# Input transpositions from TensorE to VectorE, and two groups of small products in four 64x64 tiles, in a linear-attention plus expert-mixture kernel

## The chip, the cores and the metric

One core of one Trainium2 chip. The metric is the time on the device in microseconds (us), the median of several runs. The profile names the engines PE (TensorE), PEld (TensorE's weight loads), DVE (VectorE), ACT (ScalarE), POOL (GpSimd) and SP (SyncE).

## The reference, cut to what matters

```python
# r, k, v, w, a, b: (B=4, H=8, S=768, D=40), fp32
for t in range(S):
    y[:, :, t] = einsum('bhd,bhde->bhe', rt, state)
    Sa = einsum('bhde,bhe->bhd', state, at)
    state = state * wt[:, :, None, :] - einsum('bhd,bhe->bhde', Sa, bt) \
          + einsum('bhd,bhe->bhde', vt, kt)
x = y.transpose(0, 2, 1, 3).reshape(3072, 320)
# four experts, F = 1024
p = domain_probs / (domain_probs.sum(-1, keepdims=True) + 1e-09)
for e in range(4):
    out += p[:, e:e+1] * (relu(x @ w1[e]) @ w2[e])
```

## The kernel before: the parts that matter

The 768 tokens are taken in 12 chunks of 64. Inside a chunk the recurrence becomes triangular products (E, F, C, X below), a 64x64 inverse whose 32x32 half is solved on VectorE, and a few products with the state. A **unit** is two batches of one chunk: 8 pairs of heads, 24 units. Chunks are grouped in seven **blocks** of 1, 2, 2, 2, 2, 2, 1.

The expert products of the block before are cut into pieces, and `mix(us)` puts some us' worth of them into TensorE's instruction stream. TensorE's order is fixed by hand: it is the order of the program. The order of the other engines is chosen when the kernel is built, and is fixed from then on.

Inputs come as one run of 40 floats (160 bytes) for each token, and TensorE turns them, into PSUM:

```python
by.dma_start(out=n[:, :, 0:D], in_=src[0].rearrange("h t e -> t h e"))

def turn(x):
    p = bank("p" + x)
    for j in range(NJ):                       # 4 transpositions on TensorE
        nc.tensor.transpose(out=p[:, j*P:(j+1)*P],
            in_=nat[x][:, 2*j:2*j+2, :].rearrange("p h e -> p (h e)"), identity=ident[:])
    return p
```

E and F, and C and X, are pairs of products that share the moving operand; one product of 64 rows by 128 columns does both:

```python
def triangles(u):                             # E/F
    for m in range(M):                        # M = 8
        for s in range(2):
            nc.tensor.matmul(out=pef[s][:, m*L:(m+1)*L],
                lhsT=KNT[half(s), m].rearrange("p x t -> p (x t)"), rhs=u.AE[half(s), s, m, :], ...)
# ... in step(): C/X
            nc.tensor.matmul(out=pc[s][:, m*L:(m+1)*L],
                lhsT=VST[half(s), i, j*P:(j+1)*P], rhs=u.R[half(s), m, :], ...)
```

The order of a block:

```python
def attention(b, after):
    us = b.units
    stage(us[0], 1)
    for y, u in enumerate(us):
        stage(u, 2)                           # turn NK, KN, A; scale
        if y + 1 < len(us):
            stage(us[y + 1], 1)               # turn W, scan, reciprocal of the next unit
        mix(4.3)
        stage(u, 3)                           # triangles
        mix(2.2)
        stage(u, 4)                           # natural
    ...
    solve()                                   # VectorE, 32 us or so
    mix(56)
    # ... inverse, then the steps of each chunk, then the gather for the experts
```

## Time and profile before

| | before |
|---|---|
| time, median of 3 (range) | 1390.56 us (1390.23 to 1391.24) |
| span of the profiled run | 1389.3 us |
| end of the first and the second solve on VectorE | 79.6, 198.1 us |
| TensorE after 198.1 us: occupied, idle | 1136.5, 50.0 us |

TensorE's "occupied" time is counted in its own instruction order: from the start of one record to the start of the next, less the part in which it demonstrably did nothing. I use it rather than the listed means of single products because products overlap (in the timeline quoted in the prediction the group of E/F listed with 1.89 us from 726.87 on ends 0.16 us after the next group has started, at 728.60). The profile lines themselves are in the prediction below; one more is needed later, the queue of the input loads (packets, MB, share of 16 DMA engines).

### The profile page before, as it was taken

What the parts mean: (1) busy time and instruction counts of PE and PEld (TensorE: products, weight loads), DVE (VectorE), ACT (ScalarE), POOL (GpSimd) and SP (SyncE); (2) the same over time, 40 slices, a digit from 0 to 9 for tenths busy, and PEclk for the clock granted to TensorE, in tenths of its full rate; (3) what the DMA queues carried; (4) which work ended last, traced back from release to release, by engine and by line L of the source; (5) the groups of instructions that cost most, each with busy time, mean ns of one, the idle gap of its engine ahead of it and who ended that gap; (6) DMA issues with size and microseconds to landing.
All of it is one profiled execution on the core that took longest, in us unless ns stands there. A gap on an engine that the chain in (4) does not pass through costs nothing.

```text
span 1389.3 us, 26523 instructions
## 1 busy us (share of the span) xinstructions
PE 1250.1 (90%) x11680; PEld 869.5 (63%) x11680; DVE 624.7 (45%) x898; ACT 283.9 (20%) x609; POOL 88.7 (6%) x123
## 2 busy tenths in 40 slices
PE   5076779999999989999989999989999989899998
PEld 5075658866567666567666567666567765466676
DVE  8854573566403657303566403465603369011000
ACT  2022212132131131131122131122131221120111
POOL 4000010000100000100000100000100001000010
PEclk8568889999999999999999999989999999899999
DMA  7214634555223554243453333464214440414363
GB/s 123 54 21 73 110 84 97 116 110 109 76 49 87 103 102 90 48 87 87 95 111 62 76 78 68 95 126 75 66 50 93 90 110 12 102 39 105 95 151 86
DMA packets 216722, 118.42 MB, mean 85 GB/s; under 512 B 181985, under 2 KB 200481, under 8 KB 216609
## 3 DMA queue, kind: packets, MB, share of 16 engines
q0 software_dynamic: 17600, 73.46, 21.4%
q1 hardware_dynamic: 194720, 42.63, 18.1%
q8 instruction: 92, 1.51, 0.5%
q10 hardware_dynamic: 4288, 0.66, 0.4%
q14 instruction: 22, 0.17, 0.0%
HBM read 108.84 MB, written 7.86 MB: 84 GB/s over the span
## 4 chain that ended last, share of the span: by engine, by line
PE 74%; DVE 13%; DMA 6%; issue 5%; ACT 1%; SPq 1%; POOL 0%; DVEq 0%; POOLq 0%; ACTq 0%
PE ph L481 27%; PE po L493 23%; DVE tmp L287 3%; PE pef L223 3%; PE pc L414 3%; DMA natW<-in_w_dram 3%; DMA w1s<-in_moe_w_dram 2%; PE py L426 2%; DVE Y L291 2%; PE pa L375 2%; PE pSN L347 2%; PE py L432 2%; PE pt L385 2%; PE pVST L347 2%; DVE Xl L291 1%
## 5 line engine op out<-in xcount | busy, mean ns | idle before, releaser
L481 PE MATMUL ph<-xT,w1s 64*128 64x512 f32 (+1 forms) x2240 | 453.2, 548 | 31.7 <-DVE osb L502 9.4
L493 PE MATMUL po<-w2s,hs 128*128 128x320 f32 x1536 | 435.0, 441 | 0.0
L493 PEld LDWEIGHTS po<-w2s,hs 128*128 128x128 f32 x1536 | 292.1, 193 | 124.3 <-issue 10.4
L481 PEld LDWEIGHTS ph<-xT,w1s 64*128 64x128 f32 x2240 | 223.7, 193 | 223.7 <-issue 194.6
L487 ACT ACTIVATE hs<-ph 128x512 f32<-128x512 f32 (+1 forms) x224 | 111.0, 534 | 687.3 <-PE ph L481 686.7
L502 DVE SCALAR_TENSOR_TENSOR osb<-po,gate,osb 128x320 f32<-128x320 f32 x72 | 39.5, 550 | 339.5 <-PE po L493 339.1
L199 DVE RECIPROCAL GI<-G 128x512 f32<-128x512 f32 x24 | 80.5, 3353 | 0.8
L467 POOL DMA_DIRECT2D w1s<-in_moe_w_dram x56 | 37.8, 679 | 571.9 <-PE ph L481 571.7
L230 ACT COPY F<-pef 32x512 f32<-32x512 f32 x96 | 45.1, 469 | 102.2 <-PE pef L223 101.0
L353 DVE COPY SN<-pSN 128x512 f32<-128x512 f32 x24 | 16.6, 692 | 108.4 <-PE pSN L347 108.4
L232 DVE TENSOR_TENSOR AE<-pef,mask 64x512 f32<-64x512 f32 x48 | 33.1, 689 | 64.9 <-ACT F L230 64.6
L471 POOL DMA_DIRECT2D w2s<-in_moe_w_dram x28 | 26.0, 928 | 538.2 <-PE po L493 530.4
L223 PEld LDWEIGHTS pef<-AE,KNT 64*128 64x128 f32 x768 | 50.0, 198 | 14.6 <-issue 10.3
L223 PE MATMUL pef<-AE,KNT 64*128 64x64 f32 x768 | 51.5, 282 | 5.0 <-DVE KNT L210 3.5
L176 PE MATMUL pW<-ident,natW 128*128 128x128 f32 x96 | 18.8, 330 | 34.8 <-DMA natW<-in_w_dram 29.4
L414 PEld LDWEIGHTS pc<-R,VST 64*128 64x128 f32 x768 | 44.9, 188 | 5.6 <-issue 4.1
L414 PE MATMUL pc<-R,VST 64*128 64x64 f32 x768 | 45.7, 272 | 1.1 <-DVE RV__99 L407 1.1
L325 PE MATMUL pi<-F 32*32 32x32 f32 x768 | 14.2, 195 | 32.1 <-DVE F L310 32.1
L420 DVE TENSOR_TENSOR CX<-pc,mask 128x512 f32<-128x512 f32 x48 | 30.7, 686 | 27.3 <-PE pc L414 27.2
L192 ACT COPY w_shift<-pW 128x512 f32<-128x512 f32 x24 | 14.0, 585 | 130.7 <-PE pW L176 121.2
L437 DVE TENSOR_TENSOR Yo<-py,G 128x512 f32<-128x512 f32 x24 | 16.6, 692 | 53.2 <-PE py L432 53.2
L176 PEld LDWEIGHTS pW<-ident,natW 128*128 128x128 f32 x96 | 12.8, 166 | 38.2 <-issue 32.4
(104 smaller groups left out, 1097.1 us busy)
## 6 DMA issues: line engine op xcount, KB each, us to landing
w1s<-in_moe_w_dram POOLq DMA_DIRECT2D x56, 640.0 KB, 7.6
w2s<-in_moe_w_dram POOLq DMA_DIRECT2D x28, 1280.0 KB, 7.1
xT<-yD SPq DMA_DIRECT2D x24, 320.0 KB
natW<-in_w_dram SPq DMA_DIRECT2D x48, 80.0 KB
natA<-in_a_dram SPq DMA_DIRECT2D x48, 80.0 KB
yD<-Yo SPq DMA_DIRECT2D x48, 80.0 KB
out_dram<-osb SPq DMA_DIRECT2D x48, 80.0 KB
natR<-in_r_dram SPq DMA_DIRECT2D x44, 80.0 KB
```

The source lines that it names most:

```text
L199: nc.vector.reciprocal(out=u.GI[:], in_=u.G[:, :, 1:L + 1])
L223: nc.tensor.matmul(out=pef[s][:, m * L:(m + 1) * L], lhsT=KNT[half(s), m].rearrange("p x t -> p (x t)"), rhs=u.AE[half(s), s, m, :], start ...
L230: nc.scalar.copy(out=F_[r, u.m, 0:L - z * Q], in_=cut(pef[s][r])[:, :, z * Q:L])
L287: nc.vector.tensor_tensor(out=m, in0=in0[:, :, None, :].to_broadcast([P, n0, n1, nr]), in1=in1[:, None, :, :].to_broadcast([P, n0, n1, nr] ...
L291: nc.vector.tensor_reduce(out=out, in_=m, axis=AX.X, op=ALU.add, negate=negate)
L347: nc.tensor.transpose(out=p[:, j * P:(j + 1) * P], in_=t[:, i, j].rearrange("p s d -> p (s d)"), identity=ident[:],)
L414: nc.tensor.matmul(out=pc[s][:, m * L:(m + 1) * L], lhsT=VST[half(s), i, j * P:(j + 1) * P], rhs=u.R[half(s), m, :], start=True, stop=True,)
L467: nc.gpsimd.dma_start(out=w1s[half(d)], in_=moe_w1[e, :, d * (F // 2):(d + 1) * (F // 2)].rearrange("(k p) f -> p k f", p=64),)
L481: nc.tensor.matmul(out=ph[d][:, 0:n], lhsT=w1s[half(d), k_, f * P:(f + 1) * P], rhs=xT[half(d), k_, 0:n], start=(k_ == 0), stop=(k_ == NK ...
L487: nc.scalar.activation(out=hs[-1][1][:, 0:n], in_=ph[d][:, 0:n], func=ACTF.Relu)
L493: nc.tensor.matmul(out=po[:, 0:DM], lhsT=h[:, tt * P:(tt + 1) * P], rhs=w2s[:, f, :], start=(x == 0), stop=(x == NF - 1),)
L502: nc.vector.scalar_tensor_tensor(out=osb[tt][:], in0=po[:, 0:DM], scalar=sc, in1=osb[tt][:], op0=ALU.mult, op1=ALU.add,)
```

## The change

The intent is to take work off TensorE, which was busy 90% of the span.

1. Inputs are loaded as runs of four tokens (640 bytes; two tokens and 320 bytes in the blocks of one chunk), straight into the rows from which VectorE's transposition in squares of 32x32 turns them. As 40 is more than 32, each input is loaded twice, the second copy shifted by 32 elements. TensorE's 20 input transpositions per unit, their PSUM banks and ScalarE's copies of two of the five (W and R) go.
2. E/F and C/X are written as 64x64 products in four tiles of the array, twice as many instructions.
3. The order changes: whole pairs of units are prepared at once; the turns of the next block are ordered behind the solve, which then runs uninterrupted; from the fourth load of a block on, loads are issued after the previous block's gather; the credits of `mix` are new (14 ahead of each pair's E/F, 50 beside the solve).

```diff
+    def turn(x, b, p, out):
+        nq = 2 * b.n
+        n = natural_tile(b.n)
+        end = M * nq * D
+        b.loads += 1
...
+            if b.before and b.loads > 3:
+                order.enter_context(tc.issue_after(b.before.gathered))
             for s in range(2):
+                src = srcs[x][s][2*p:2*p+2, s::2, b.t, :].rearrange("i j (r q) e -> r (i j) (q e)", q=nq)
+                for d in range(2):
+                    by = nc.scalar if b.cs[0] == p == 0 and s == 1 else nc.sync
+                    o = Q * (1 - d)
+                    by.dma_start(out=n[SL[s]+Q*d : SL[s]+Q*d+Q, o:o+end].rearrange("r (x e) -> r x e", e=nq*D), in_=src)
+        with ExitStack() as order:
+            if solved:
+                order.enter_context(tc.issue_after(solved[-1]))
+            nc.vector.transpose(
+                out=out.rearrange("p c m (r q) -> p m q c r", q=nq),
+                in_=n[:, Q:Q+end].rearrange("p (m q e) -> p m q e", q=nq, e=D)[:, :, :, 0:Q].rearrange(
+                    "p m q (c r) -> p m q c r", c=b.n))
...
-                nc.tensor.matmul(
-                    out=pef[s][:, m*L:(m+1)*L], lhsT=KNT[half(s), m].rearrange("p x t -> p (x t)"),
-                    rhs=u.AE[half(s), s, m, :], start=True, stop=True)
+                for x in range(2):
+                    nc.tensor.matmul(
+                        out=pef[s][half(x), m*L:(m+1)*L], lhsT=KNT[rows(s), m, x, :],
+                        rhs=u.AE[rows(s), s, m, :], start=True, stop=True)
...
-            nc.tensor.matmul(out=pc[s][:, m*L:(m+1)*L], lhsT=VST[half(s), i, j*P:(j+1)*P],
-                rhs=u.R[half(s), m, :], start=True, stop=True)
+            for x in range(2):
+                nc.tensor.matmul(out=pc[s][half(x), m*L:(m+1)*L],
+                    lhsT=VST[rows(s), i, j*P+x*L : j*P+(x+1)*L], rhs=u.R[rows(s), m, :], start=True, stop=True)
...
     def attention(b, after):
+        for p in range(NP):
+            if p >= b.early:
+                decays(b, p)                  # turn W, scan, reciprocal
+            scaled(b, p)                      # turn NK, KN, A; scale
+            if not start:
+                turned_r(b, p)
+            mix(14)
+            for u in pairs[p]:
+                triangles(u)
             mix(4.3)
+            for u in pairs[p]:
+                natural(u)
...
         solve()
+        if start:                             # first block: the rest waits until the solve is done
+            for p in range(NP):
+                turned_r(b, p)
+            decays(after, 0)
...
-        mix(56)
+        mix(50)
```

Cut: the multiplications now read SBUF for pairs of units, G has two buffers of pairs instead of four of units, the mask is built by GpSimd, the accumulator `osb` has four buffers instead of five.

## The prediction

> **What bounds the kernel now.** I read the page first: the busy times, the 40 slices and the costliest groups.
>
> ```profile
> PE 1250.1 (90%) x11680; PEld 869.5 (63%) x11680; DVE 624.7 (45%) x898; ACT 283.9 (20%) x609; POOL 88.7 (6%) x123
> ...
> PE   5076779999999989999989999989999989899998
> ...
> DVE  8854573566403657303566403465603369011000
> ```
>
> TensorE is busy for 1250 of 1389 us. It is idle in the first seven slices (243 us); after that each slice is 80% to over 90% full. VectorE works in bursts and never fills a late slice. Next I read the view of stretches, to separate the start from the steady part.
>
> ```profile
> 35.00:70.00 35.00, 1.09 (x4) 0.71 (x4) 28.42 (x50) 0.58 (x1) 0.00 (x0) 0.50 0.26 50
> ...
> 140.00:175.00 35.00, 27.69 (x202) 22.28 (x200) 19.62 (x43) 8.34 (x21) 2.27 (x3) 0.85 0.62 114
> ...
> 600.00:780.00 180.00, 169.85 (x1648) 115.81 (x1646) 95.61 (x136) 40.10 (x84) 8.73 (x11) 0.97 0.42 85
> ```
>
> The columns after the length are PE, PEld, DVE, ACT and POOL busy, then clock and DMA share. So there are two regimes. **At the start** the first 32x32 solve runs alone on VectorE (TensorE works 1.1 of 35 us). **Later**, TensorE is 94% busy and any TensorE time taken out of its instruction order shortens the run. The timeline shows what the affected groups occupy in that order; I take start to start of the next group, not the listed mean, because matmuls overlap.
>
> ```profile
> 726.87 1.89 PE L223 MATMUL pef<-AE,KNT 64*128 64x64 f32 x32
> 728.60 4.51 PE L481 MATMUL ph<-xT,w1s 64*128 64x512 f32 x20
> ...
> 733.98 0.60 PE L176 MATMUL pR<-ident,natR 128*128 128x128 f32 x4
> 734.41 0.60 PE L176 MATMUL pNK<-ident,natNK 128*128 128x128 f32 x4
> ...
> 825.34 1.13 PE L375 MATMUL pa<-RV__98,AE 128*64 128x40 f32 x32
> 826.29 1.11 PE L375 MATMUL pa<-RV__99,AE 128*64 128x40 f32 x32
> ```
>
> Four input transposes take 734.41 - 733.98 = 0.43 us; the 32 E/F products of a unit 1.73 us (54 ns each; 1.94 us in a slower place). The C/X products (L414) take 3.6 us for two units. The view of waits, of TensorE alone, also shows TensorE waiting for inputs, because an input must land before its transposition can leave TensorE's fixed order:
>
> ```profile
> PE pi L325 <- DVE F L310: 32.1, 1, 32.1
> PE pW L176 <- DMA natW<-in_w_dram: 29.4, 10, 9.3
> PE ph L481 <- DVE osb L502: 9.4, 1, 9.4
> ...
> PE pR L176 <- DVE AE L232: 7.0, 8, 1.7
> ```
>
> [...]individual records in L414 start in pairs 6 ns apart, the next pair 112 ns after the first (128 columns[...]); with 64-column weights (L385, L375) the pairs come every 58 ns[...]. [...]No group of the kernel before uses four at once, but L426 runs two row tiles together and L375 two column tiles together (start gaps of 7 and 51 ns), so both directions are seen to overlap. [...]1024 elements in 1.92 us (the solve's transposition of F)[...]. I use 1.9 to 2.1 us.
>
> **The change, part by part.** A unit is two batches of one 64-token chunk; there are 24 of them, in seven blocks (1, 2, 2, 2, 2, 2, 1 chunks).
>
> *Transpositions leave TensorE.* Five inputs x 0.435 us = 2.17 us per unit, with their ScalarE copies (w_shift and R, 28 us in all), which bound nothing.
>
> *Four tiles.* E/F goes from 16 pairs x 112 ns = 1.79 us to 16 groups of four x 58.5 ns = 0.94 us per unit; the instruction count doubles, to 15 ns apart, which L325 nearly shows already (128 in 2.15 us, 16.8 ns). C/X gains the same. Together 1.7 us per unit. So TensorE loses 3.9 us per unit, 93 us over all 24 units, but only those after the start count in full.
>
> *VectorE gains.* 50 transpositions of 1024 elements at 2.0 us and 20 of 512 at 1.05 us = 121 us. The multiplications read SBUF in place of PSUM and are paired: 24 of 1024 elements at 1.22 us (rate of the solve's 1024-element products) against 48 at 0.68; AE similar. Reciprocals (80 us) and scans (30 us) stay. VectorE goes from 625 to about 740 us, 58% of the new span: no bound on average.
>
> *DMA.* Each input is loaded twice, 19.7 to 39.3 MB, but in runs of 640 bytes (four tokens) rather than 160, so about 72,000 packets in place of 123,000. The hardware queue's share should stay near 16 to 18%. I count no gain or loss.
>
> *Start up to the end of the second block's solve (0 to 198 us in the timeline).* The first solve ran from 31.8 to 79.6 us, with two scans, two reciprocals and a 5 us wait for the next block's W inside. The change orders the next turns behind the solve: it then lasts about 34 us (35.2 less four other evictions of 0.5 us in the steady block at 744.7). VectorE's new chain before it (turn 1.05, scan 1.24, reciprocal 3.35, two turns, product 1.22, turn, two AE at 0.69, all twice) puts its start near 32 us, as before, so it ends near 66. The steps take 27 us, as before, plus some 4 us of waits behind the postponed W and R work: gather near 97 us (before: about 107). Block two then needs on VectorE: turns 14, scan and reciprocal 9, products 10, masks 3 and 33 us of solve, plus evictions and landing: solve ends near 175 us instead of 198. Gain **23 us**.
>
> *From there to the end.* TensorE loses 18 units x 3.9 + 4 units x 0.86 (C/X only) = **74 us**. Idle there was about 55 us, 8 of some 10 us per block being input landings, which TensorE no longer waits for directly. But the new chain after a block's last step (G has two buffers, so the next W turn cannot start earlier) is turn 2 + scans 2.5 + reciprocal 6.7 + product 2.45 + turn 2 + AE 2.45 = 18 us, about 20 with evictions, against some 15 us of expert products scheduled in its shadow; the second pair is 27 us against 24. So I expect 5 to 8 us of idle per steady block in place of 10: gain **8 us**, chosen from a possible -15 to +35. The solve (34 us, under 55 us of scheduled products) has room to spare.
>
> Sum: 1390 - 23 - 74 - 8 = **1285 us**.
>
> **Rivals.** *VectorE becomes the bound.* For it: 120 us of VectorE work per steady block, in runs of 20 to 27 us that TensorE must wait for, and step evictions (0.5 to 0.7 us) queue behind 6.7 us reciprocals. Against: the period stays near 195 us, and the schedule now gives 14 units of credit before each pair. If all such runs were uncovered, 20 us per block more: 1370 to 1390 us. *Column tiles do not load beside each other when row tiles do too.* For: no group before runs four at once. Against: the pair gaps above. Then E/F and C/X stay at 1.8 us per unit: 37 us lost, about 1320 us. *The waits vanish altogether*, as no transposition sits in TensorE's order any longer and the credits were retuned: 25 to 35 us better, about 1255 us. *Doubled bytes delay expert weights*: the last blocks already wait 9 us for w1s; 5 to 15 us worse.
>
> **Range and chances.** 1285 us; low 1250 from the vanishing waits with a little more at the start, high 1322 from the failed four-tile overlap or 7 more us of idle per block. To stay within 2% (above 1363 us) VectorE would have to eat nearly everything saved: 0.05; slower 0.02; faster 0.93.
>
> **What would show it.** In the profile after: about 11,700 + 1536 - 480 matmuls, PE busy near 1160 us; E/F and C/X near 15 ns from start to start (30 refutes); STREAM_TRANSPOSE of 128x1024 near 2.0 us, VectorE near 740 us; the first solve ended near 66 us and the second near 175; TensorE's waits for natW gone and waits of E/F for VectorE's AE or KNT there, 2 to 5 us each. The prediction fails if those waits exceed 15 us per block, or a transposition takes over 3 us.

1390 - 23 - 74 - 8 = 1285 us is worked out from figures (pairs of records 112 and 58 ns apart, 0.43 us for four transpositions, 1.92 us for 1024 elements on VectorE). That two pairs can run side by side as four tiles was the author's estimate from those gaps; nothing in the kernel before shows four at once.

## More of the kernel before

From the page of the kernel before:

```profile
q1 hardware_dynamic: 194720, 42.63, 18.1%
```

## The result

| | before | after | difference |
|---|---|---|---|
| time, median of 4 (range) | 1390.9 (1390.23 to 1396.01) | 1310.99 (1308.56 to 1317.53) | |
| ratio, 95% interval | | 0.9425 (0.9385 to 0.9466) | |
| span of the profiled run | 1389.3 | 1309.8 | -79.5 |
| end of the second solve | 198.1 | 188.4 | -9.7 |
| TensorE occupied after that | 1136.5 | 1073.8 | -62.7 |
| TensorE idle after that | 50.0 | 42.9 | -7.1 |

A ratio is the mean time of one kernel's runs over that of the other's of the same rounds, so it is not quite the ratio of the medians quoted here. The three last rows add up to the difference of the spans: -9.7 - 62.7 - 7.1 = -79.5.

The page of the kernel after: busy times and counts, two rows of the 40 slices, and the queue of the input loads.

```profile
PE 1169.0 (89%) x12736; PEld 805.1 (61%) x12736; DVE 720.9 (55%) x966; ACT 260.4 (20%) x561; POOL 92.7 (7%) x128
...
PE   2067679979899989999989999989999999999998
...
DVE  7995883579803388913389913369913355702000
...
q1 hardware_dynamic: 144192, 62.13, 23.0%
```

TensorE lost 81 us of busy time (1250.1 to 1169.0) with 1056 more instructions, and VectorE gained 96. VectorE now has full slices, about one per block, and after the start the slices beside them on TensorE still read 9: its bursts lie mostly beside products. The input queue moves half as much again with a quarter fewer packets, and its packets took a larger share of time, 23.0 against 18.1%.

The view of stretches of the kernel after (length; PE, PEld, DVE, ACT, POOL busy; clock; DMA share; GB/s), for the same three stretches as in the prediction:

```profile
35.00:70.00 35.00, 2.60 (x90) 2.52 (x92) 33.39 (x55) 1.92 (x6) 1.89 (x2) 1.00 0.50 104
...
140.00:175.00 35.00, 28.75 (x276) 22.80 (x276) 30.70 (x56) 8.66 (x22) 2.28 (x3) 0.79 0.42 95
...
600.00:780.00 180.00, 173.97 (x1833) 114.33 (x1832) 113.39 (x142) 36.84 (x75) 9.79 (x13) 0.97 0.47 109
```

In the steady 180 us TensorE is busier than before (173.97 against 169.85): it does the same work in a shorter period. VectorE has gone from 95.6 to 113.4 us. In the first stretch VectorE is nearly full (33.4 of 35 us, 28.4 before): the solve runs without interruption. (This trace holds no record of the clock before 75.95 us, so the 1.00 of the first stretch is not a measurement.)

The timeline of TensorE after, for E/F and C/X (start, length in us; engine; line; operation; tiles; count; wait):

```profile
117.88 2.10 PE L277 MATMUL pef<-AE__113,KNT 40*64 40x64 f32 x128
119.91 2.43 PE L543 MATMUL ph<-xT,w1s 64*128 64x256 f32 x20
...
221.68 2.15 PE L472 MATMUL pc<-R,VST 40*64 40x64 f32 x128
223.75 2.43 PE L543 MATMUL ph<-xT,w1s 64*128 64x256 f32 x20
```

From 117.88 to 119.91 us 128 records of E/F take 2.03 us, 15.9 ns each; C/X takes 2.07 us, 16.2 ns. After the first four, single records start in fours, 6 to 7 ns apart, each four 58 ns behind the one before; in the kernel before, the records of L375 and L385 came in pairs 58 ns apart. So all four tiles run at once. (Each fp32 product appears as two records, so 128 records are the 64 products of two units.)

The waits of TensorE after (waited us, times, longest):

```profile
PE pef L277 <- DVE AE__113 L260: 39.7, 12, 14.1
...
PE ph L543 <- DMA xT<-yD: 16.4, 7, 6.9
PE pef L277 <- DVE AE__114 L260: 16.4, 7, 12.0
PE ph L543 <- DMA w1s<-in_moe_w_dram: 9.2, 5, 3.1
...
PE pVST L403 <- ACT VS__107 L451: 5.8, 1, 5.8
```

The waits for `natW` are gone. In their place E/F waits for AE, which is the end of VectorE's new chain. Expert products also wait longer for the gather (xT, 7.8 us before, 16.4 now). That chain at the boundary of a steady block, from the timeline of VectorE after:

```profile
460.72 2.01 DVE L203 STREAM_TRANSPOSE G<-nat__75 128x1024 f32<-128x1024 f32 x1
463.18 2.35 DVE L239 TENSOR_TENSOR_SCAN G<-G,first 128x520 f32<-128x520 f32 x2
465.56 6.55 DVE L243 RECIPROCAL GI<-G 128x1024 f32<-128x1024 f32 x1
...
472.39 2.35 DVE L253 TENSOR_TENSOR KNT<-KNT,GI 128x1024 f32<-128x1024 f32 x2
...
477.14 2.47 DVE L260 TENSOR_TENSOR AE__113<-AT,G 40x1024 f32<-40x1024 f32 x2
```

From 460.72 to 479.61 us is 18.9 us; and TensorE at the end of it, with the clock of the same time from the view of stretches:

```profile
478.50 0.33 PE L277 MATMUL pef<-AE__113,KNT 40*64 40x64 f32 x4 [3.02 <-DVE AE__113 L260]
479.75 3.43 PE L277 MATMUL pef<-AE__113,KNT 40*64 40x64 f32 x115 [0.92 <-DVE AE__113 L260]
...
485.18 10.71 PE L543 MATMUL ph<-xT,w1s 64*128 64x512 f32 x40
```

```profile
478.00:489.00 11.00, 8.02 (x138) 5.61 (x140) 7.31 (x8) 3.76 (x8) 0.00 (x0) 0.53 0.88 216
489.00:500.00 11.00, 11.00 (x60) 5.55 (x60) 10.93 (x5) 3.48 (x8) 0.00 (x0) 1.00 0.35 87
```

TensorE waited 3.02 + 0.92 us, and a granted clock of a half was recorded for 10.2 us (478.7 to 489.0 us): 115 records of E/F in 3.43 us are 29.8 ns each, against 15.9 ns at 117.88 us, where the granted clock was 1.00. So the wait costs more than its own length: E/F is the group that runs right behind it.

Two more blocks show the same: waits of 2.45 and 0.77 us go with a granted clock of 0.5 for 10.2 us (676.69 to 686.93 us), waits of 3.13 and 0.92 us with 6.8 us of it (878.08 to 884.91). At 676.69 us the record of the clock falls 0.24 us before the first wait, of 2.45 us, ends at 676.93, and so before the second wait began. (The profile models where a product ends, so the length of a wait is not exact.) Before the second pair of another block E/F waited 0.63 and 0.92 us (from 310.06 us on), and the granted clock stayed at 1.00.

### The profile page after: what moved, and what is told of

Its sections match the earlier page's. It is cut to its first block, busy times and chain, and to the rows that moved or that the text cites. A ratio compares the mean times of both kernels' runs of the same rounds, so it can differ in the third digit from the quotient of the medians.

```text
span 1309.8 us, 28541 instructions
## 1 busy us (share of the span) xinstructions
PE 1169.0 (89%) x12736; PEld 805.1 (61%) x12736; DVE 720.9 (55%) x966; ACT 260.4 (20%) x561; POOL 92.7 (7%) x128
## 3 DMA queue, kind: packets, MB, share of 16 engines
q1 hardware_dynamic: 144192, 62.13, 23.0%
## 4 chain that ended last, share of the span: by engine, by line
PE 63%; DVE 14%; issue 13%; DMA 6%; POOL 2%; SPq 1%; ACT 1%; DVEq 0%; POOLq 0%
PE ph L543 24%; PE po L555 21%; DMA w1s<-in_moe_w_dram 2%; PE pef L277 2%; PE pa L432 2%; PE pc L472 2%; PE pSN L403 2%; PE pt L442 2%; PE pVST L403 2%; DVE tmp L342 2%; PE py L484 1%; PE py L490 1%; DMA xT<-yD 1%; DVE AT L203 1%; DVE KNT L203 1%
## 5 line engine op out<-in xcount | busy, mean ns | idle before, releaser
L543 PE MATMUL ph<-xT,w1s 64*128 64x512 f32 (+1 forms) x2240 | 465.8, 555 | 32.6 <-DMA xT<-yD 16.4
L543 PEld LDWEIGHTS ph<-xT,w1s 64*128 64x128 f32 x2240 | 250.2, 196 | 215.6 <-issue 184.0
L243 DVE RECIPROCAL GI<-G 128x1024 f32<-128x1024 f32 (+1 forms) x14 | 78.9, 5638 | 0.3
L277 PE MATMUL pef<-AE__113,KNT 40*64 40x64 f32 x896 | 24.3, 273 | 41.3 <-DVE AE__113 L260 39.7
L277 PEld LDWEIGHTS pef<-AE__113,KNT 40*64 40x64 f32 x896 | 21.9, 183 | 47.4 <-DVE AE__113 L260 26.8
L495 DVE TENSOR_TENSOR Yo<-py,G 128x512 f32<-128x512 f32 x24 | 16.5, 687 | 51.1 <-PE py L490 41.2
L342 DVE TENSOR_TENSOR tmp<-Y,Tl 128x1024 f32<-128x1024 f32 (+2 forms) x49 | 35.7, 729 | 1.7
L346 DVE TENSOR_REDUCE Y<-tmp 128x32 f32<-128x256 f32 (+3 forms) x49 | 35.5, 724 | 1.7
L346 DVE TENSOR_REDUCE Xl<-tmp 128x32 f32<-128x128 f32 (+3 forms) x49 | 35.5, 724 | 1.6
L409 DVE COPY SN<-pSN 128x512 f32<-128x512 f32 x24 | 16.5, 689 | 34.9 <-PE pSN L403 34.9
L381 PEld LDWEIGHTS pi<-F 32*32 32x32 f32 x768 | 13.4, 111 | 35.1 <-issue 30.9
L286 DVE TENSOR_TENSOR AE__113<-pef,mask 64x512 f32<-64x512 f32 x28 | 19.3, 689 | 26.4 <-ACT F L284 21.9
L472 PEld LDWEIGHTS pc<-R,VST 40*64 40x64 f32 x1536 | 25.0, 135 | 12.3 <-issue 12.2
```

The source lines that it names most:

```text
L243: nc.vector.reciprocal(out=b.GI, in_=G[:, :, :, 1:L + 1])
L277: nc.tensor.matmul(out=pef[s][half(x), m * L:(m + 1) * L], lhsT=KNT[rows(s), m, x, :], rhs=u.AE[rows(s), s, m, :], start=True, stop=True,)
L342: nc.vector.tensor_tensor(out=m, in0=in0[:, :, None, :].to_broadcast([P, n0, n1, nr]), in1=in1[:, None, :, :].to_broadcast([P, n0, n1, nr] ...
L346: nc.vector.tensor_reduce(out=out, in_=m, axis=AX.X, op=ALU.add, negate=negate)
L472: nc.tensor.matmul(out=pc[s][half(x), m * L:(m + 1) * L], lhsT=VST[rows(s), i, j * P + x * L:j * P + (x + 1) * L], rhs=u.R[rows(s), m, :], ...
L543: nc.tensor.matmul(out=ph[d][:, 0:n], lhsT=w1s[half(d), k_, f * P:(f + 1) * P], rhs=xT[half(d), k_, 0:n], start=(k_ == 0), stop=(k_ == NK ...
```

## The experiments

**Theory.** Both removals pay as predicted. What is missing against the prediction (26 us) should lie (a) at the start, where the second block's A comes late, and (b) in the waits of E/F for VectorE's chain and the slow clock behind them. **Rivals.** The four tiles give nothing by themselves; the transpositions alone do all; VectorE's load is the new limit; the doubled bytes cost time.

All runs were timed in three rounds. The kernel before had medians of 1390.7, 1393.0, 1391.3 and 1393.0 us. Unless said otherwise a result was correct.

### 1. The four tiles alone, in the kernel before

```diff
-  nc.tensor.matmul(out=pef[s][:, m*L:(m+1)*L], lhsT=KNT[half(s), m].rearrange("p x t -> p (x t)"), ...)
+  for x in range(2):
+      nc.tensor.matmul(out=pef[s][half(x), m*L:(m+1)*L], lhsT=KNT[half(s), m, x, :], ...)
   # and C/X in the same way; all else as before
```

> The kernel before with one part of the change alone: E/F and C/X as 64x64 products, four tiles at once; the transpositions stay on TensorE. Theory (four tiles overlap fully and the time counts where TensorE is the bound): start to start falls from 56-58 to 15-17 ns per product, 1.7 us per unit over 22 units, so about 37 us less: 1354 us against 1391. Rival 1 (the two column tiles of one row group do not load beside each other here): 29-31 ns per product, time unchanged within 5 us. Rival 2 (the four-tile saving is only worth something together with the shorter waits of the changed kernel): TensorE busy falls by 37 us but idle rises by as much, time within 10 us of before.

Measured: 1368.4 us (1365.1 to 1372.6), ratio 0.9837 (0.9813 to 0.9861). Its timeline of TensorE:

```profile
890.66 1.16 PE L224 MATMUL pef<-AE,KNT 64*64 64x64 f32 x64
891.75 4.58 PE L495 MATMUL po<-w2s,hs 128*128 128x320 f32 x16
```

Its waits of TensorE for inputs (waited us, times, longest):

```profile
PE pW L176 <- DMA natW<-in_w_dram: 30.5, 9, 13.1
PE pKN L176 <- DMA natW<-in_w_dram: 11.3, 2, 6.0
PE pKN L176 <- DMA natKN<-in_b_dram: 10.8, 2, 6.4
```

and those of the kernel before that the prediction does not show:

```profile
PE pKN L176 <- issue: 7.5, 2, 4.1
...
PE pKN L176 <- DMA natKN<-in_b_dram: 5.8, 2, 3.4
```

The 64 records of one unit take 1.09 us, 17.1 ns each, against 54 to 60 ns for the 64x128 records of the kernel before: the tiles overlap here too. Over the whole run TensorE's occupied time fell by 38.6 us, but its idle time rose by 12.5. The idle time before pKN, the transposition of KN, went from 13.3 us (5.8 for a load, 7.5 that the profile puts down to nothing, "issue") to 22.1 us, all for loads (10.8 and 11.3): the faster TensorE reached these transpositions before their data had landed. So the tiles alone give 22 us, and a third of what they take off TensorE turned into waits, most of them for inputs.

### 2. All but the tiles: the changed kernel with 64x128 products

```diff
-  for x in range(2):
-      nc.tensor.matmul(out=pef[s][half(x), m*L:(m+1)*L], lhsT=KNT[rows(s), m, x, :], ...)
+  nc.tensor.matmul(out=pef[s][:, m*L:(m+1)*L], lhsT=KNT[rows(s), m].rearrange("p x t -> p (x t)"), ...)
   # and C/X in the same way
```

> The changed kernel with E/F and C/X put back as 64x128 products in pairs; transpositions stay on VectorE. If the two parts add up, this costs about 35 us against the changed kernel (1346 us) and, with the run of the four tiles alone, the gains sum to the 80 us of the whole. If E/F sits behind a VectorE wait whatever its length, the E/F half is hidden at the waits of the first pair but not elsewhere: 20-25 us (1333 us).

Measured: 1344.1 us (1342.9 to 1345.0), ratio 0.966 (0.9646 to 0.9675). Against the kernel before, the transpositions gain about 47 us together with the new order and credits, which this run keeps; no run separates these. On top of them the tiles gain 33. The two parts done alone sum to 22 + 47 = 69 us, and done together they give 80. The traces show where the difference comes from (11 us in the medians, 6 between the profiled runs), and it is not from fewer waits. Between this run and the changed kernel TensorE's occupied time falls by 53.0 us over the whole run (38.6 in run 1) and its idle time rises by 20.9 (12.5 in run 1). The tiles take more off here because E/F is slower in the new order. Run 2's timeline, in the block whose E/F is shown above:

```profile
487.82 6.84 PE L276 MATMUL pef<-AE__113,KNT 40*128 40x64 f32 x61 [0.60 <-DVE AE__113 L260]
494.28 1.16 PE L541 MATMUL ph<-xT,w1s 64*128 64x512 f32 x1
```

From 487.82 to 494.28 us 61 records take 106 ns each, at a granted clock of 0.5 (recorded from 485.3 to 499.0 us). In the kernel before a record took 54 to 60 ns in the steady blocks. After the second solve E/F occupies 49.8 us here and 33.2 in the kernel before, so there is more for the tiles to shorten (to 26.2 in the changed kernel).

### 3. Other credits: more products ahead of the first pair's E/F

```diff
-  mix(14)
+  mix(14.5 if p else 18)
...
-  mix(50)
+  mix(45)
```

> The changed kernel with the credits of expert products moved: 18 before the first pair's E/F (was 14), 14.5 before the second's, 45 beside the solve (was 50). Theory (VectorE's chain of W turn, scans, reciprocal, product, A turn, AE after a block's last step outlasts the scheduled products by 3-5 us, and the idle time then drops the clock for 7-10 us): the 3 us waits of E/F for AE in the steady blocks vanish, the clock stays up there, 5-8 us per block over four or five blocks: 1280-1295 us. Rival (the wait only moves: the same products are then missing beside the solve, or the expert evictions queue behind VectorE): within 5 us of 1311.

Measured: 1308.6 us (1306.4 to 1309.4), ratio 0.9404 (0.9386 to 0.9421). The difference to the changed kernel is 2 us and within the intervals. Its waits of TensorE:

```profile
PE pef L277 <- DVE AE__113 L260: 26.0, 4, 14.1
PE ph L543 <- DMA w1s<-in_moe_w_dram: 24.3, 10, 6.5
```

The first-pair waits went from 12 to 4 and from 39.7 to 26.0 us, as the theory said; but the waits for the first expert weights went from 9.2 to 24.3 us, and the half-clock time after the second solve did not fall (68.7 us before, 69.9 with these credits). One wait was traded for another.

The traces show where that other wait comes from. The timeline of GpSimd in the kernel after:

```profile
551.78 1.94 POOL L370 MEMSET XT<- 32x1024 f32 x2 [25.96 <-DVE XT L367]
553.67 1.35 POOL L529 DMA_DIRECT2D w1s<-in_moe_w_dram  x2
```

and TensorE some us later:

```profile
562.57 8.00 PE L543 MATMUL ph<-xT,w1s 64*128 64x512 f32 x36 [1.46 <-DMA w1s<-in_moe_w_dram]
```

The memset of XT needs the end of VectorE's solve, and here GpSimd waited 26 us for it (25.96 us). The issue of the next expert's weights stands right behind it in GpSimd's instructions: it went out at 553.67 us, when the solve had ended, and its two copies landed after 5.9 and 8.1 us, when TensorE already wanted them (it waited 1.46 us). In three blocks of the kernel before the two are apart: there the issue was released by TensorE, 8 us after the memset:

```profile
777.90 1.94 POOL L314 MEMSET XT<- 32x1024 f32 x2 [11.52 <-DVE XT L312]
786.23 1.35 POOL L467 DMA_DIRECT2D w1s<-in_moe_w_dram  x2 [6.38 <-PE ph L481]
```

That this order costs the waits is read from the traces; no run moved the memset, so it is not tested.

### 4. A third buffer for G

The prediction held that G's two buffers keep the next W turn from starting before the block's last step.

```diff
-  G = held(b, p, "G", [M, L + 1], 2)
+  G = held(b, p, "G", [M, L + 1], 3)
   # Yo takes CX's buffers, to make room
```

> The changed kernel with three buffers of G (Yo shares the buffers of CX to make room). Theory (the next block's W turn must wait for the last reader of the old G, which starts the exposed VectorE chain only at the block's end): W turn, scans and reciprocal, 11 us, move ahead of the block's end, the waits of E/F for the first pair's AE vanish in the steady blocks, 5-8 us per block: 1280-1295 us. Rival (a 6.5 us reciprocal in the middle of the steps delays the step's own evictions as it did in the first block, where TensorE waited 5.8 us for VS): waits of pVST, pc or py for VectorE appear, time within 10 us of 1311 or above.

Measured: 1328.9 us (1327.4 to 1330.3), ratio 0.9551 (0.9537 to 0.9565): **slower** than the changed kernel by 18 us. The timelines of VectorE and TensorE show why:

```profile
563.76 6.50 DVE L243 RECIPROCAL GI<-G 128x1024 f32<-128x1024 f32 x1
...
572.83 1.92 DVE L565 SCALAR_TENSOR_TENSOR osb<-po,gate,osb 128x320 f32<-128x320 f32 x4
```

```profile
573.43 7.06 PE L544 MATMUL ph<-xT,w1s 64*128 64x512 f32 x22 [11.05 <-DVE osb L565]
```

With a buffer free, the turn, scans and reciprocal of the next W were placed directly behind the solve, in one burst of 17 us with two more turns and a product. The evictions of expert results (osb) queued behind it, four at once at 572.83, and TensorE stood 11 us for a PSUM bank. These waits are 43.3 us in six places. So the two buffers of G do hold the chain back, and that is where it is harmless. The theory "the chain should simply start earlier" falls; it has to start in between.

### 5. The second block's A and R loaded ahead of the gather

```diff
-  if b.before and b.loads > 3:
+  if b.before and b.loads > (5 if b.before.before is None else 3):
```

> The changed kernel, but the second block may issue its A and R loads before the first block's gather (limit 5 loads in place of 3, for that block alone). In the changed kernel VectorE sat idle for 10 us (101.7 to 111.8 us) until A had landed, and the second solve ended 13 us later than predicted. Theory (that landing is what the second block's chain hangs on): A's turn and AE move into the steps, the second solve ends 6-10 us earlier, the run is 5-9 us shorter (1302-1306 us). Rival (TensorE's expert products of the first block, which cannot start before the gather has landed, set the pace there): second solve earlier, but the time within 2 us.

Measured: 1302.6 us (1301.9 to 1303.0), ratio 0.935 (0.9331 to 0.937); the second solve ended at 182.3 us instead of 188.4. In the kernel after, VectorE stood idle for this load at the start of block two:

```profile
111.84 2.02 DVE L203 STREAM_TRANSPOSE AT<-nat__74 128x1024 f32<-128x1024 f32 x1 [10.11 <-DMA nat__74<-in_a_dram]
```

Cause (a) is shown: 8 us of the missing 26.

### 6. Products without use ahead of E/F, to keep the clock up

```diff
   # before triangles, in every block but the first, for the first pair
+  if not start and p == 0:
+      pw = bank("pwarm")
+      for _ in range(24):
+          nc.tensor.matmul(out=pw[:, 0:P], lhsT=ident, rhs=ident, start=True, stop=True)
```

> The changed kernel with 24 idle products of 128x128x128 (about 2.6 us, results never read) put into TensorE's order just before the E/F of each block's first pair, where it waited 2-4 us and the clock then fell to 0.5 for 7-10 us in three of the steady blocks. Theory (the clock loss is a real part of the cost of these waits): the clock stays up there, E/F returns from 27 to 16 ns per product and the products after it to full speed: 2-4 us gained in each of three or four blocks, 1300-1306 us. Rival (the fall of the clock costs nothing that is not waited for anyway, or the window has fallen before): 1311 us or up to 6 us more, as the idle products push where there is no wait.

Measured: 1319.9 us (1318.1 to 1320.5), ratio 0.9473 (0.9452 to 0.9494), 7 to 9 us slower. In the three blocks whose first pair had waited, E/F went from 6.3 to 6.5 us per block to 4.7 to 5.5, and in two of them the half-clock time, from one solve's end to the next, fell from 10.2 to 3.4 us; in the other it stayed at 17.1. But the products were mis-sized: each is two records of 115 ns, so 24 take 5.5 us (the expected 2.6 us was an estimate; it fits one record of 109 ns for each, as the transpositions of the kernel before took), more than the wait they were to fill, and they stood in blocks that had no wait.

### 7. A and R loaded once only (a wrong result)

```diff
-  for d in range(2):
+  for d in range(1 if x in "AR" else 2):
   # GpSimd fills the rows of the missing copy with 0.45 at the start
```

> Wrong on purpose: of A and R only the first copy of the two is loaded (the rows of dimensions 32 to 39 then hold what the buffer held before). It asks what the doubled bytes and issues of these loads cost. Theory (the landing of A behind the gather costs its latency and the order of the queue, not its bytes): 1-2 us per block at most, time within 6 us of 1311. Rival (doubling the input bytes is what delays A and the expert weights): A lands 3-4 us earlier in every block, 1290-1300 us.

Measured: 1298.4 us (1297.5 to 1300.3), ratio 0.9325 (0.9301 to 0.9349); the result is wrong (relative error 1.10). That is 12.6 us faster, although its start lasted 5 us longer for the filling. The rival "doubled bytes cost time" is thus supported: some 13 us or more for two of five inputs, where I had counted none for all. The run also issues half as many loads of A and R, so bytes and issues are not told apart. The gain is spread over the blocks (1.6 to 6 us from the end of one solve to the end of the next), in small waits and in the half-clock time (68.7 to 57.9 us after the second solve); the queue's share fell from 23.0 to 20.5%. Which transfers the added loads delay I could not tell from the trace, which has no landing times for SyncE's loads; that stays open. The expert weights are not delayed in flight: the two copies of w1s issued behind each solve from the third on landed 5.7 to 5.9 and 7.9 to 8.3 us after their issue in the changed kernel, and 5.7 to 5.8 and 7.8 to 8.2 us after it here.

### 8. The third buffer of G, with the chain placed in between

```diff
   # as run 4, and in turn():
+  if x == "W" and p == 0 and b.before and b.before.n == 2:
+      order.enter_context(tc.issue_after(b.before.units[1].done))   # behind the first chunk's Yo
   # in decays():
-  nc.vector.reciprocal(out=b.GI, in_=G[:, :, :, 1:L + 1])
+  for c in range(b.n):
+      nc.vector.reciprocal(out=b.GI[:, c], in_=G[:, c, :, 1:L + 1])
...
-  if b.before and b.loads > 3:
+  if b.before and b.loads > 4:               # A ahead of the gather
```

> Third G buffer again, but with what made it lose taken away: the next block's W turn is ordered behind the output of the block's first chunk and not right behind the solve, where the 17 us burst of VectorE work held the expert evictions and TensorE lost 11 us in three blocks; the reciprocals are issued one chunk at a time (3.35 us); and A, the fourth load, no longer waits for the gather, which had become the limit of the first pair's E/F there. Theory (G, A's load and the eviction order together are what makes TensorE wait in a steady block): waits of E/F for the first pair fall below 1 us, 4-6 us per block: 1285-1300 us. Rival (the work only blocks other evictions, now those of the second chunk's steps): waits of pVST, pc, py for VectorE in their place, 1308-1325 us.

Measured: 1293.9 us (1285.4 to 1297.3), ratio 0.928 (0.9241 to 0.9319). In the steady blocks the first-pair waits are gone. New, smaller ones came: of the VST transposition for VS (12.2 us in 5 places) and of pd for VST (7.1 us in 3). Of the 16.5 us between the profiled runs only 1.7 lie before the end of the second solve (186.7 us against 188.4), and some 15 us are gained in the blocks after it, where cause (b) lies. The run also moves A's load in every block and splits the reciprocals, so the share of each is not shown. The buffers are those of run 4, so they were not what made run 4 slow; the trace there shows the chain's place in VectorE's order (a burst of 17 us ahead of the evictions, and 11.05 us of waiting on TensorE).

### 9. Twelve useless products, only in the third to sixth block

```diff
+  if p == 0 and b.n == 2 and b.before.n == 2:   # range(12) in place of 24
```

> The idle products again, rightly sized: in the run before each of the 24 products turned out to be two records of 115 ns, 5.5 us in all, longer than the wait that they should fill, and they also stood in two blocks where E/F waits for nothing. Now 12 products (2.8 us), and only in the four blocks (the third to the sixth) that follow a block of two chunks. Theory (the clock's fall after the wait is a cost of its own): E/F of the first pair runs at 16-17 ns per product there, at the same place in time, and the products after it at full speed: 2-3 us per block in three of the four blocks, 1303-1307 us. Rival (the clock's fall is hidden by the next wait): 1309-1313 us.

Measured: 1313.3 us (1307.8 to 1316.5), ratio 0.9436 (0.9406 to 0.9466): no difference. E/F is again faster, by 1.0 to 1.8 us per block; from 478 to 489 us the granted clock was 0.84, against 0.53 in the changed kernel. The trace shows an even trade after the second solve: idle time falls by 6.6 us (42.9 to 36.3) and E/F by 4.5 us (26.2 to 21.7), but the useless products occupy 11.6 us. So the slow clock behind the wait costs time in E/F, and filling the wait costs as much as it saves; what the slow clock alone is worth is not shown.

### 10 and 11. Combinations

```diff
   # best_a: run 8 with
+  if b.before and b.loads > 5:               # A and R ahead of the gather
   # best_b: best_a with
+  mix(18 if p else 9)                        # in place of 14
+  mix(51)                                    # in place of 50
```

> Third G buffer, split reciprocals and ordered W turn as in the run that gave 1294 us, and now A and R (the fourth and fifth loads) of every block may be issued before the gather. In that run VectorE waited up to 10 us for R's landing at a block's start, with other work behind it. Theory: those waits go, the second block's solve ends 4 us earlier as in the run with early A and R there; 1283-1291 us. Rival (more loads ahead of the outputs on the same queue delay the gather, and the expert products wait for it instead): within 3 us of 1294.

Measured: 1294.7 us (1291.1 to 1298.3), ratio 0.9315 (0.9289 to 0.9341). The second solve ended at 182.3 us as in run 5, yet there is no gain over run 8; the reason is not shown.

> As the run before it in this call, with the credits 9 ahead of the first pair's E/F, 18 ahead of the second's and 51 beside the solve (14, 14, 50 before), since the first pair is now ready early and the waits of up to 3 us are at the second pair. Theory: waits at the second pair go too, 2-4 us per block: 1275-1287 us. Rival (the expert products become due earlier or later than their weights land, or the first pair waits again): within 4 us of the run before it or slower.

Measured: 1290.1 us (1289.3 to 1295.0), ratio 0.928 (0.9256 to 0.9305). Its waits of TensorE:

```profile
PE pef L280 <- DVE AE__113 L263: 26.1, 4, 14.1
PE pVST L406 <- ACT VS__107 L454: 11.8, 5, 5.1
```

The four waits of E/F left in the first line belong to the start and block two. This run and run 8, both at 0.928, and run 10 are the fastest, and their intervals overlap; the first two beat the kernel before by 7.2% and the changed kernel by about 1.5% (0.928 over 0.9425).

### 12. A turned twice

This doubles one part of VectorE's new load: 14 more transpositions, 22.9 us.

```diff
-  nc.vector.transpose(out=..., in_=...)
+  for _ in range(2 if x == "A" else 1):
+      nc.vector.transpose(out=..., in_=...)
```

> The changed kernel with A's transposition on VectorE issued twice (same result): 14 more transpositions, 22.8 us of VectorE work in all, two in each block, each in the chain that E/F waits for. Theory (VectorE is the bound just there, though it is busy for 55% of the span): both of a two-chunk block's reach TensorE, 3 to 4 us in each of five blocks and 0.7 us twice at the start: 1325-1332 us, nearly all of the 22.8 us. Rival (VectorE has room on average, and expert products fill in): within 4 us of 1311.

Measured: 1316.5 us (1312.6 to 1318.3), ratio 0.9446 (0.9414 to 0.9477). The medians differ by 5.5 us, about a quarter of what was added, and the intervals overlap. Its waits of TensorE:

```profile
PE pef L278 <- DVE AE__113 L261: 47.0, 12, 14.9
...
PE ph L544 <- DMA w1s<-in_moe_w_dram: 3.6, 5, 1.9
```

Each first-pair wait of a steady block grew by the full 2 us (3.02 to 5.11, 2.45 to 4.44, 3.13 to 5.23), but the waits for w1s shrank from 9.2 to 3.6 us. VectorE is not the bound; its chain is one of two or three things that end within a few us of each other.

## Why the prediction was right, and where it was off

It said 1285 us (1250 to 1322) and faster with 0.93; the time was 1311.0. The mechanism held for TensorE: its occupied time fell, and waits for VectorE's chain took the place of waits for inputs. The miss of 26 us lies in a wait at the start that was not priced, and in the sizes of terms, some of which cancelled by luck.

- **Start, -23 predicted, -9.7 measured: the step that failed.** The first solve was to run from 32 to 66 us; it ran from about 35.3 to 69.2. Its length of 34 us was right, its start 3 us late. The gather was then issued at 103.9 us instead of 97: I allowed 4 us for waits behind the postponed W and R work, and one step alone waited 5.8 us for VS (the last line of the waits after), whose eviction stood behind a 6.5 us reciprocal. The remaining 6 us lie behind the gather: block two's A is loaded only after it, and VectorE stood 10.1 us for it, where the prediction had some 9 us for evictions and landing together (175 less 97 less 69 of VectorE work) and no separate price for this ordering, which the diff shows. Run 5 loads A earlier: the second solve ends 6.1 us earlier, and the run gains 8 us.
- **TensorE's occupied time, -74 predicted, -62.7 measured.** The parts, measured after the second solve: input transpositions -48.2 (predicted 18 x 2.17 = 39); C/X -16.8 (predicted 22 units x 0.86 = 18.9); E/F -7.0 (predicted 18 x 0.86 = 15.5); expert products +5.4; the rest about +4. The tile spacing of 15 ns was right, 15.9 to 16.2 ns. The mis-sized term is E/F: I priced it at the full clock. In the changed order it runs right behind the one wait of the block, at about half the clock, so its mean spacing after the second solve is 22.8 ns. (What the prediction calls the 32 E/F products of a unit are the 32 records of 16 products; its sums are not touched by this.) Runs 6, 8 and 9 show that it is the clock: where the wait is filled or gone, the 128 records of a first pair take 2.0 to 2.3 us in these three blocks, in place of 3.9 to 4.2.

The transpositions were mis-sized by the same step, the other way: 59 of the 360 records took over 180 ns instead of 109, 40 of them where the granted clock stood at 0.5 behind a wait, as here in the kernel before (0.22 us each):

```profile
718.03 1.08 PE L176 MATMUL pKN<-ident,natKN 128*128 128x128 f32 x4 [3.42 <-DMA natKN<-in_b_dram]
718.91 1.06 PE L176 MATMUL pA<-ident,natA 128*128 128x128 f32 x4
```

So the slow stretch behind a wait moved from the transpositions to E/F. The two errors, 9 us too little and 8.5 us too much, cancel, and that is luck.

- **Idle time, -8 predicted, -7.1 measured.** Right in kind: waits for natW gone, waits of E/F for AE of 2 to 4 us in their place, a chain of 18.9 us (predicted 18). The sum is right in part by luck. From one solve's end to the next, from the second on, TensorE was idle for 7.7, 10.6, 10.2, 10.1 and 4.1 us before and for 12.9, 11.8, 6.2, 8.1 and 3.9 us after: the predicted 5 to 8 us came only in two, and in the first two it rose (8.1 us of the 12.9 were waits for the gather, 5.1 of the 11.8 for w1s). What evens it out is the last block, where 7.4 us of waits for w1s are gone, which the prediction did not count.
- **VectorE.** 1024-element transpositions of 2.0 us were right; the 512-element ones took 0.65 to 0.72 us, not 1.05, and VectorE came to 720.9 us instead of 740. So twice the elements took nearly three times as long here, while a VectorE product of 1024 elements took 1.22 us against 0.69 us for 512. The two forms of transposition differ in their strides as well; which difference matters no run here shows.
- **DMA.** 72,000 packets for the inputs was right in effect (194,720 to 144,192 on the queue), but "no gain or loss" was not: the share rose from 18.1 to 23.0%, where I had said 16 to 18. Run 7 shows a cost of some 13 us for the second copies of A and R alone, a part of which sits in the waits and the clock already counted above.
- **Rivals.** Failing overlap is refuted by the 15.9 ns. VectorE as the bound is refuted by run 12. Delayed weights exist (9.2 us for w1s), but in the trace they come from GpSimd's order (the 26 us at the memset) rather than from the bytes: run 7, with fewer bytes, has the same landing times, though its waits for w1s came to 5.7 us.

## What to carry to other kernels

Here work taken off TensorE, which bounds the kernel, did not pay in full where something else ended within a few us of it; two halves of a change gave 22 and 47 us alone and 80 together. The worth of one half depended on the other: the tiles took 38.6 us off TensorE in the old order and 53.0 in the new, where E/F ran slower, and in both about a third or more of it turned into waits (12.5 and 20.9 us). Before pricing an ordering ("after the gather", "behind the solve"), look for what is held by it in each engine's instructions: here a load on SyncE (VectorE stood 10.1 us for A), a small eviction behind a 6.5 us reciprocal (TensorE waited 5.8 us for VS), weights behind a memset on GpSimd that waited 26 us. And an earlier start of a long burst on a helper engine can cost more than it gains: the same third buffer made the kernel slower by 18 us when the chain ran as one burst, and, with the chain placed later, in pieces, and A's load earlier, faster by 17.
